# Eight orders for the up projection's matmuls and four for the down projection's, from the second tile on

## The chip, the cores and the metric

The kernel runs on one core of one Trainium2 chip. The metric is the time of one execution in microseconds of device time; lower is better. An execution consists of a linear attention (a decayed outer-product state over 768 tokens, four batches, eight heads) and, behind it, a gated feed-forward network over all 3072 tokens.

## What is computed

The reference, cut to what matters here:

```python
for t in range(S):                                   # S = 768 tokens, D = 48 channels a head
    cur = einsum('bhd,bhe->bhde', u * k[t], v[t])
    y[t] = einsum('bhd,bhde->bhe', r[t], state + cur)
    state = w * state + einsum('bhd,bhe->bhde', k[t], v[t])
x = y as (B * S, H * D)                              # 3072 x 384
gate = 1 / (1 + exp(-(x @ w_gate)))                  # 384 -> 1536
out = (gate * (x @ w_val)) @ w_out                   # 1536 -> 384
```

All of it is float32. The kernel reaches that accuracy on TensorE with a rounded type (F32R): every number is kept as a high part and a low part, and a product is three matmuls, low weights by high data, high by high, and high by low. `PASS = ((1, 0), (0, 0), (0, 1))` on line 480 lists the three as (part of the weights, part of the data).

## The kernel before

The 768 tokens are cut into 12 chunks of 64, and two chunks of the four batches make a tile of 512 columns, so there are six tiles. The attention works through 24 groups (a chunk and one half of the heads each, `GROUPS`), and each group writes its quarter of a tile's `xt`. The feed-forward network takes a tile in 12 blocks of 128 hidden units (`NF = 12`, index `f`). A block consists of

- `up(f)`, line 492: for the gate (`g = 0`) and then for the value (`g = 1`) nine matmuls (three `kt`, the thirds of the 384 inputs, by three passes) that add up in one bank of PSUM, 18 matmuls of 512 columns in all, on line 502;
- `sigmoid(f)` on ScalarE (line 511) reads the gate's bank, `product(f)` on VectorE (line 515) reads the value's bank and multiplies, `h_high(f)` on ScalarE (line 520) rounds to the high part, and `h_low(f)` on GpSimd (line 524) makes the low part;
- `down(f)`, line 532: nine matmuls (line 540) that add to three accumulators, three passes `k` by three parts of the output; in the sixth tile the third part is two pieces of 256 columns, so it has twelve.

All engines take their instructions in the order in which the program writes them. For the first tile that order stands in the string `START`. From the second tile on it is the loop at the end: for each block `i` in turn `up`, `sigmoid` and `product`; then, in the blocks that `SLOTS` names, one group of attention, `apply(n)` (line 368) and what follows it; then `h_high`, `h_low`; and then `finish(i - 1)`, the down projection of the block before. TensorE therefore sees up of block i, in 16 blocks the attention's small matmuls, down of block i - 1, up of block i + 1, and so on.

PSUM has eight banks. Two hold attention scores (`two_banks`), three the accumulators, and three are the pool `ring` (line 67), handed out in turn by `one_bank()` (line 79). `up` takes two of the ring's banks, first the gate's and then the value's, and `apply` takes two for its output:

```python
yb[n] = one_bank(), one_bank()        # line 371, in apply(n)
o = one_bank()                        # line 497, in up(f), for g = 0 and then for g = 1
```

With three banks A, B, C in turn, an up projection in A (gate) and B (value) is followed by an up projection in C and A, or, in the 16 blocks of `SLOTS`, by `apply` in C and A and then an up projection in B and C. An instruction that writes a bank waits until the last reader of the bank's former content is done. The first small matmul of `apply` writes the first of its two banks and the second one the other (`from_state`, through `into_y` on line 320). The slots are `f` = 4, 6, 8, 10 in the second tile and `f` = 1, 4, 7, 10 in the third to the fifth; the sixth has none.

Of the kernel before, what the change touches and what calls it, by code (L numbers as in the profile page):

```python
# [18 lines left out]
DM, DF = H * D, 1536  # L19
P = 128  # L20
# [3 lines left out]
NF = DF // P  # L24
# [33 lines left out]
def rwkv_then_moe(ctx: ExitStack, tc: tile.TileContext, wd, ch, tk, rt, ut, wt, rk0, vn0, wd0, out):  # L58
    nc = tc.nc
# [16 lines left out]
    def two_banks():  # L76
        return ps.tile([P, 2, 512], F32, name="sc")

    def one_bank():
        return ring.tile([P, 512], F32, name="ring")  # L80
# [12 lines left out]
    w = wu[:, 0]  # L93
# [162 lines left out]
    xt, dec, ga, yb, kv = {}, {}, {}, {}, {}  # L256
# [223 lines left out]

    PASS = ((1, 0), (0, 0), (0, 1))

    class Moe:
        def __init__(self, x, acc, cols, last=None):
            self.x, self.acc, self.cols = x, acc, cols
            c = self.cols
            self.parts = [(0, acc[0], c, c), (1, acc[1], c, c), (2, acc[2], c, c)]
            if last is not None:
                left, right = slice(0, CT), slice(CT, 2 * CT)
                self.parts[2:] = [(2, acc[2], left, left), (2, last, left, right)]  # L490
            self.pair, self.sg, self.h = {}, {}, {}

        def up(self, f):
            w = whi[f], wlo[f]
            self.pair[f] = []
            for g in range(2):
                o = one_bank()
                self.pair[f].append(o)
                k = 0
                for kt in range(3):  # L500
                    for a, b in PASS:
                        nc.tensor.matmul(  # L502
                            o[:, self.cols], w[a][:, g * DM + kt * P : g * DM + (kt + 1) * P],
                            self.x[:, kt, b, self.cols], start=(k == 0), stop=(k == 8),
                        )
                        k += 1

        def sigmoid(self, f):
            c, sg = self.cols, hp.tile([P, 512], F32, name="sg")
# [22 lines left out]
        def down(self, f):  # L532

            h, w = self.h.pop(f), (whi[f], wlo[f])
            todo = [(k, part) for k in range(3) for part in self.parts]
            if f == NF - 1:
                todo = [(k, part) for part in self.parts for k in range(3)]
            for k, (d, acc, to, cols) in todo:
                a, b = PASS[k]
                nc.tensor.matmul(  # L540
                    acc[:, to], w[a][:, 2 * DM + d * P : 2 * DM + (d + 1) * P],
                    h[:, b, cols], start=(f == 0 and k == 0 and self.cols.start == 0),
                    stop=(f == NF - 1 and k == 2),
                )

    def accumulators():
        return [pacc.tile([P, 512], F32, name=f"acc{d}") for d in range(3)]
# [35 lines left out]
    moes, accs = {}, {}  # L583

    def moe_of(it):
        ti, h, f = it
        if ti not in accs:
            accs[ti] = accumulators()
        if (ti, h) not in moes:
            cols = (slice(0, CT), slice(CT, 2 * CT), slice(0, 2 * CT))[h]  # L590
            last = two_banks()[:, 0] if ti == len(TILES) - 1 else None
            moes[ti, h] = Moe(xt[ti], accs[ti], cols, last)
        return moes[ti, h]

    def finish(i):
        ti, h, f = items[i]
        moe_of(items[i]).down(f)
        if f == NF - 1:
            if ti == len(TILES) - 1:
                store_last(moe_of(items[i]), TILES[ti][0])  # L600
            else:
                store(accs[ti], slice(TILES[ti][0], TILES[ti][-1] + 1))
# [13 lines left out]
        "o0v": lambda j: rest_of_weights(0, HALVES[j], nc.vector),  # L616
        "Rv": lambda n: queries(n, nc.vector), "Tv": lambda n: token_keys(n, nc.vector),
        "qv": lambda i: moe_of(items[i]).h_low(items[i][2], nc.vector),
        "U": lambda i: moe_of(items[i]).up(items[i][2]),
        "g": lambda i: moe_of(items[i]).sigmoid(items[i][2]),  # L620
# [4 lines left out]
    for step in START.split():  # L625
        name, _, arg = step.partition(".")
# [3 lines left out]
    last = len(GROUPS) - 1  # L630
# [18 lines left out]
    for i in range(n0, len(items)):  # L649
        ti, h, f = items[i]  # L650
# [44 lines left out]
    with tc.If(bad != 0):  # L695
        with ExitStack() as g:
# [65 lines left out]
            x = gp.tile([P, 3, 2, 512], F32R, name="xgr")  # L762
# [116 lines left out]
```

## Time and profile before

| what | value |
|---|---|
| runs of the kernel | 539.41, 539.42 and 540.52 us, median 539.42 |
| profiled execution, first to last instruction | 538.6 us |
| TensorE busy with matmuls | 519.2 us, 96% |
| TensorE loading weights (beside matmuls) | 426.9 us, 79% |
| VectorE, ScalarE, GpSimd busy | 218.3, 171.8, 175.0 us |
| matmuls of line 502 (up) | 1332, of which 1260 have 512 columns |
| matmuls of line 540 (down) | 666 |

The profiled execution's span is 0.8 us below the median of the timed runs. Busy time of TensorE is modelled: a matmul of 512 columns is shown 0.39 us long, but the next one starts 0.23 us after it. Where the text needs TensorE's pace it takes the time that 18 or 9 matmuls in a row occupy in the chain of waits, not the shown duration. `xN` behind a row is the number of instructions in it; a row of several begins with the first one's start and ends with the last one's end.

### The profile page before, as it was taken

What the parts mean: (1) busy time and instruction counts of PE and PEld (TensorE: products, weight loads), DVE (VectorE), ACT (ScalarE), POOL (GpSimd) and SP (SyncE); (2) the same over time, 40 slices, a digit from 0 to 9 for tenths busy, and PEclk for the clock granted to TensorE, in tenths of its full rate; (3) what the DMA queues carried; (4) which work ended last, traced back from release to release, by engine and by line L of the source; (5) the groups of instructions that cost most, each with busy time, mean ns of one, the idle gap of its engine ahead of it and who ended that gap; (6) DMA issues with size and microseconds to landing.
All of it is one profiled execution on the core that took longest, in us unless ns stands there. A gap on an engine that the chain in (4) does not pass through costs nothing.

```text
span 538.6 us, 12067 instructions
## 1 busy us (share of the span) xinstructions
PE 519.2 (96%) x5268; PEld 426.9 (79%) x5268; DVE 218.3 (41%) x379; ACT 171.8 (32%) x358; POOL 175.0 (32%) x156
## 2 busy tenths in 40 slices
PE   4879999999999999999999999999999999999996
PEld 3769878788788887888888888888888887888885
DVE  7798999942343342432423414313414311111111
ACT  5576654522132232231332222222322212221121
POOL 3353330002814444234145144144242311111120
PEclk9999999999999999999999999999999999999999
DMA  8886903053022213220303402203300001100001
GB/s 324 314 301 239 382 2 99 16 204 128 2 86 86 70 48 141 85 84 3 95 3 104 145 7 79 67 28 106 144 1 16 12 1 19 60 0 1 0 1 63
DMA packets 15707, 48.03 MB, mean 89 GB/s; under 512 B 2369, under 2 KB 5057, under 8 KB 14241
## 3 DMA queue, kind: packets, MB, share of 16 engines
q1 hardware_dynamic: 15360, 46.81, 25.2%
q8 instruction: 43, 0.70, 0.5%
q10 hardware_dynamic: 288, 0.39, 0.2%
q14 instruction: 16, 0.12, 0.1%
HBM read 40.12 MB, written 4.72 MB: 83 GB/s over the span
## 4 chain that ended last, share of the span: by engine, by line
PE 91%; DVE 4%; DMA 3%; ACT 1%; issue 0%; SPq 0%; DVEq 0%; ACTq 0%
PE ring L502 55%; PE acc L540 27%; PE ring L320 5%; PE sc L348 2%; DMA toks<-in_tk 1%; DMA chan<-in_ch 1%; PE sc L403 1%; DMA wr<-in_wt 1%; DVE score L362 1%; PE sc L540 1%; DVE wf L243 1%; DVE wf L244 1%; DVE wx L253 0%; ACT wf L236 0%; DVE wf L242 0%
## 5 line engine op out<-in xcount | busy, mean ns | idle before, releaser
L502 PE MATMUL ring<-xt,wx 128*128 128x512 f32 (+1 forms) x1332 | 317.1, 392 | 2.1 <-ACT wx L250 1.7
L502 PEld LDWEIGHTS ring<-xt,wx 128*128 128x128 f32 x1332 | 247.4, 191 | 57.5 <-ACT wx L250 1.9
L524 POOL TENSOR_TENSOR h<-sg,h 128x512 fp32r<-128x512 f32 (+1 forms) x68 | 91.8, 1350 | 332.4 <-ACT h L520 326.5
L540 PE MATMUL acc<-h,wx 128*128 128x512 f32 (+1 forms) x666 | 160.9, 383 | 0.0
L515 DVE TENSOR_TENSOR sg<-ring,sg 128x512 f32<-128x512 f32 (+1 forms) x74 | 50.0, 676 | 272.7 <-PE ring L502 272.7
L540 PEld LDWEIGHTS acc<-h,wx 128*128 128x128 f32 x666 | 119.6, 188 | 24.3
L511 ACT ACTIVATE sg<-ring 128x512 f32<-128x512 f32 (+1 forms) x74 | 43.4, 586 | 181.2 <-PE ring L502 181.2
L520 ACT CAST h<-sg 128x512 fp32r<-128x512 f32 (+1 forms) x74 | 45.3, 612 | 109.0 <-DVE sg L515 109.0
L422 ACT ACTIVATE state<-state,every 112x96 f32<-112x96 f32 x80 | 23.5, 363 | 26.7 <-PE ring L320 26.7
L460 DVE TENSOR_TENSOR xt<-ring,xt 112x256 fp32r<-112x256 f32 (+1 forms) x52 | 19.9, 418 | 26.9 <-ACT xt L456 26.9
L301 POOL TENSOR_TENSOR dec<-chan,every 128x512 f32<-128x512 f32 x20 | 23.8, 1190 | 13.8 <-PE ring L320 5.9
L362 DVE COPY_PREDICATED score<-masks,sc 128x512 f32<-128x512 int32 x32 | 23.8, 743 | 0.9
L456 ACT CAST xt<-ring 112x256 fp32r<-112x256 f32 (+1 forms) x52 | 17.1, 372 | 17.2 <-PE ring L320 15.6
L320 PE MATMUL ring<-score,toks 64*64 64x64 f32 (+1 forms) x768 | 18.6, 230 | 4.0 <-DVE score L362 2.0
L311 POOL TENSOR_TENSOR toks<-toks,tabn 128x384 f32<-128x384 f32 x18 | 19.7, 1093 | 0.0
L320 PEld LDWEIGHTS ring<-score,toks 64*48 64x48 f32 (+1 forms) x768 | 15.3, 133 | 5.2 <-POOL dec L301 1.9
L250 ACT CAST wx<-wf 128x1152 fp32r<-128x1152 f32 (+1 forms) x13 | 14.1, 1084 | 15.1 <-DVE wf L244 15.1
L244 DVE SCALAR_TENSOR_TENSOR wf<-wr,wf 128x1152 int32<-128x1152 int32 (+1 forms) x13 | 18.4, 1415 | 0.5
L320 PEld LDWEIGHTS ring<-dec,state 48*48 48x48 f32 (+1 forms) x704 | 12.0, 127 | 7.4 <-issue 6.7
L348 PE MATMUL sc<-dec,chan 48*64 48x64 f32 x768 | 17.6, 231 | 0.1
L289 POOL TENSOR_TENSOR dec<-dec,toks 128x384 f32<-128x384 f32 x16 | 16.3, 1016 | 1.2
L243 DVE SCALAR_TENSOR_TENSOR wf<-wr,wf 128x1152 int32<-128x1152 int32 (+1 forms) x13 | 16.5, 1266 | 0.5
(62 smaller groups left out, 253.0 us busy)
## 6 DMA issues: line engine op xcount, KB each, us to landing
wr<-in_wt SPq DMA_DIRECT2D x11, 1152.0 KB, 8.7
chan<-in_ch SPq DMA_DIRECT2D x24, 512.0 KB, 4.5
toks<-in_tk SPq DMA_DIRECT2D x24, 400.0 KB, 4.9
out_y<-wf SPq DMA_DIRECT2D x16, 256.0 KB, 2.3
dec<-in_rt SPq DMA_DIRECT2D x16, 192.0 KB, 2.6
xt<-xt SPq DMA_DIRECT2D x30, 64.0 KB, 2.3
wr<-in_wt SPq DMA_DIRECT2D x2, 576.0 KB, 5.2
xt<-xt SPq DMA_DIRECT2D x12, 32.0 KB, 4.9
```

The source lines that it names most:

```text
L244: nc.vector.scalar_tensor_tensor(g, low, 29, g, ALU.logical_shift_right, ALU.bitwise_or)
L301: eng.tensor_tensor(v4(t[:, 0]), v4(chan[n][:, 0]), bc2(table_of(n)), ALU.mult)
L320: nc.tensor.matmul(yb[n][bank][64 * half : 64 * half + m, cs], lhsT, rhs, start=first, stop=stop, skip_group_check=True,)
L348: nc.tensor.matmul(sc[64 * gm : 64 * gm + 64, be ^ gm, o : o + C], kk[row, cs : cs + C], rr[row, cs : cs + C], start=True, stop=True,)
L362: nc.vector.copy_predicated(t.rearrange("q (b m i) -> q b m i", b=2, m=4), masks[:, m].bitcast(I32).unsqueeze(1).unsqueeze(1).broadcast_to ...
L422: nc.scalar.activation(st[:, p, s], st[:, p, s], AF.Copy, scale=pw[0:112, 4 * g + 2 * p + s, 64:65],)
L502: nc.tensor.matmul(o[:, self.cols], w[a][:, g * DM + kt * P : g * DM + (kt + 1) * P], self.x[:, kt, b, self.cols], start=(k == 0), stop=(k ...
L511: nc.scalar.activation(sg[:, c], self.pair[f][0][:, c], AF.Sigmoid)
L515: nc.vector.tensor_tensor(sg[:, c], self.pair.pop(f)[1][:, c], sg[:, c], ALU.mult)
L520: nc.scalar.copy(out=h[:, 0, c], in_=sg[:, c])
L524: eng.tensor_tensor(h[:, 1, c], self.sg.pop(f)[:, c], h[:, 0, c], ALU.subtract)
L540: nc.tensor.matmul(acc[:, to], w[a][:, 2 * DM + d * P : 2 * DM + (d + 1) * P], h[:, b, cols], start=(f == 0 and k == 0 and self.cols.start ...
```

## The change

`up` and `down` no longer fix the order of their matmuls. `up_order(kind)` lists the 18 matmuls of an up projection as (g, kt, pass) in one of eight orders, `down_order(kind, parts)` the matmuls of a down projection as (pass, part) in one of four. Each matmul, its weights, its data and its bank are the same as before; the first one into a bank in the new order carries `start`, the last one `stop`. Both banks of an up projection are taken at its beginning, in the same order as before.

The first tile keeps kind 0, the old order. From the second tile on the kinds change from block to block:

| tile (ti) | up kinds, f = 0 to 11 | down kinds, f = 0 to 11 | blocks with attention |
|---|---|---|---|
| 1 | 3 4 5 6 7 0 1 2 3 4 5 6 | 2 1 2 2 3 3 0 0 1 1 2 1 | 4, 6, 8, 10 |
| 2 | 6 7 0 1 2 3 4 5 6 7 0 1 | 2 2 3 3 0 0 1 1 2 2 3 1 | 1, 4, 7, 10 |
| 3 | 1 2 3 4 5 6 7 0 1 2 3 4 | 2 3 0 0 1 1 2 2 3 3 0 1 | 1, 4, 7, 10 |
| 4 | 4 5 6 7 0 1 2 3 4 5 6 7 | 0 0 1 1 2 2 3 3 0 0 1 1 | 1, 4, 7, 10 |
| 5 | 7 0 1 2 3 4 5 6 7 0 1 2 | 2 1 2 2 3 3 0 0 1 1 2 1 | none |

Up kinds 0, 2 and 3 do the whole gate before the value. Kinds 1, 4, 5, 6 and 7 mix the two: the gate's last matmul is then the 17th of the 18 in kinds 1, 5 and 6, the 16th in kind 7 and the 15th in kind 4, where it was the ninth. Down kind 0 is pass by pass, kind 1 part by part (the last block of a tile had that before and keeps it), kinds 2 and 3 are pass by pass with the passes in the orders 1, 0, 2 and 2, 1, 0. In kind 3 the low part of `h` is read first, in kind 1 by the third matmul, in kinds 0 and 2 by the last third.

```diff
+    def up_order(kind):
+        G, K = range(2), range(3)
+        if kind == 1:
+            return [(g, kt, p) for kt in K for p in PASS for g in G]
+        if kind == 2:
+            return [(g, kt, p) for g in G for p in PASS for kt in K]
+        if kind == 3:
+            return [(g, kt, p) for g in G for kt in K for p in PASS[::-1]]
+        if kind == 4:
+            return [(g, kt, p) for kt in K for g in G for p in PASS]
+        if kind == 5:
+            one = ((0, PASS[0]), (0, PASS[1]), (1, PASS[0]), (1, PASS[1]), (0, PASS[2]), (1, PASS[2]))
+            return [(g, kt, p) for kt in K for g, p in one]
+        if kind == 6:
+            return [(g, kt, p) for ps_ in (PASS[:2], PASS[2:]) for kt in K for g in G for p in ps_]
+        if kind == 7:
+            return [(g, kt, p) for ps_ in (PASS[:1], PASS[1:]) for kt in K for g in G for p in ps_]
+        return [(g, kt, p) for g in G for kt in K for p in PASS]
+
+    def down_order(kind, parts):
+        if kind == 1:
+            return [(k, part) for part in parts for k in range(3)]
+        ks = {2: (1, 0, 2), 3: (2, 1, 0)}.get(kind, (0, 1, 2))
+        return [(k, part) for k in ks for part in parts]
+
+    UP_OF = [[0] * NF] + [[(f + 3 * ti) % 8 for f in range(NF)] for ti in range(1, 6)]
+    DOWN_OF = [[0] * NF] + [[(f // 2 + ti) % 4 for f in range(NF)] for ti in range(1, 6)]
...
         def up(self, f):
             w = whi[f], wlo[f]
-            self.pair[f] = []
-            for g in range(2):
-                o = one_bank()
-                self.pair[f].append(o)
-                k = 0
-                for kt in range(3):
-                    for a, b in PASS:
-                        nc.tensor.matmul(
-                            o[:, self.cols], w[a][:, g * DM + kt * P : g * DM + (kt + 1) * P],
-                            self.x[:, kt, b, self.cols], start=(k == 0), stop=(k == 8),
-                        )
-                        k += 1
+            self.pair[f] = [one_bank() for _ in range(2)]
+            seen_g = [0, 0]
+            for g, kt, (a, b) in up_order(UP_OF[self.ti][f]):
+                nc.tensor.matmul(
+                    self.pair[f][g][:, self.cols], w[a][:, g * DM + kt * P : g * DM + (kt + 1) * P],
+                    self.x[:, kt, b, self.cols], start=(seen_g[g] == 0), stop=(seen_g[g] == 8),
+                )
+                seen_g[g] += 1
...
         def down(self, f):
             h, w = self.h.pop(f), (whi[f], wlo[f])
-            todo = [(k, part) for k in range(3) for part in self.parts]
+            kind = DOWN_OF[self.ti][f]
             if f == NF - 1:
-                todo = [(k, part) for part in self.parts for k in range(3)]
+                kind = 1
+            elif f == 0 and kind:
+                kind = 2
+            todo = down_order(kind, self.parts)
```

## Rows read from the trace of the kernel before

**Rows 1.** The page: TensorE's busy time, granted clock by slices, and the chain's shares.
```profile
PE 519.2 (96%) x5268; PEld 426.9 (79%) x5268; DVE 218.3 (41%) x379; ACT 171.8 (32%) x358; POOL 175.0 (32%) x156
...
PEclk9999999999999999999999999999999999999999
...
PE 91%; DVE 4%; DMA 3%; ACT 1%; issue 0%; SPq 0%; DVEq 0%; ACTq 0%
```

**Rows 2.** Waits from 110 us on, longest first: who waited for whom, us, times, longest.
```profile
POOL h L524 <- ACT h L520: 300.4, 60, 38.3
DVE sg L515 <- PE ring L502: 269.4, 61, 5.6
ACT sg L511 <- PE ring L502: 172.8, 61, 3.6
...
PEld ring L320 <- issue: 6.2, 17, 0.4
```

**Rows 3.** The chain of waits from 262 to 304 us: start, duration, what.
```profile
266.51 2.05 PE acc L540 x9
268.57 4.19 PE ring L502 x18
...
274.81 4.20 PE ring L502 x18
279.01 0.61 PE ring L320 x28
...
293.71 2.05 PE acc L540 x9
```

**Rows 4.** The timeline of a block with attention, 253.5 to 263 us.
```profile
253.70 4.36 PE L502 MATMUL ring<-xt,wx 128*128 128x512 f32 x18
256.05 0.60 ACT L511 ACTIVATE sg<-ring 128x512 f32<-128x512 f32 x1 [2.79 <-PE ring L502]
257.99 0.54 PEld L320 LDWEIGHTS ring<-dec,state 48*64 48x64 f32 x32 [0.37 <-issue]
257.99 0.68 PE L320 MATMUL ring<-dec,state 48*64 48x64 f32 x32
258.17 0.69 DVE L515 TENSOR_TENSOR sg<-ring,sg 128x512 f32<-128x512 f32 x1 [5.56 <-PE ring L502]
...
260.55 0.76 DVE L460 TENSOR_TENSOR xt<-ring,xt 112x256 fp32r<-112x256 f32 x2 [1.57 <-ACT xt L456]
...
261.39 1.30 POOL L524 TENSOR_TENSOR h<-sg,h 128x512 fp32r<-128x512 f32 x1 [6.76 <-ACT h L520]
...
262.16 1.09 PE L502 MATMUL ring<-xt,wx 128*128 128x512 f32 x4
```

**Rows 5.** The timeline of the next block, without attention, 263 to 276.9 us.
```profile
266.35 2.22 PE L540 MATMUL acc<-h,wx 128*128 128x512 f32 x9
266.62 0.69 DVE L515 TENSOR_TENSOR sg<-ring,sg 128x512 f32<-128x512 f32 x1 [2.54 <-PE ring L502]
...
268.04 1.30 POOL L524 TENSOR_TENSOR h<-sg,h 128x512 fp32r<-128x512 f32 x1 [5.35 <-ACT h L520]
...
268.40 4.36 PE L502 MATMUL ring<-xt,wx 128*128 128x512 f32 x18
...
272.60 2.22 PE L540 MATMUL acc<-h,wx 128*128 128x512 f32 x9
```

**Rows 6.** The timeline around 39 us: TensorE waits there for ScalarE.
```profile
37.83 1.15 ACT L250 CAST wx<-wf 128x1152 fp32r<-128x1152 f32 x1 [0.68 <-DVE wf L244]
...
38.99 0.30 PEld L502 LDWEIGHTS ring<-xt,wx 128*128 128x128 f32 x2 [1.85 <-ACT wx L250]
39.02 0.47 PE L502 MATMUL ring<-xt,wx 128*128 128x256 f32 x2 [1.68 <-ACT wx L250]
```

**Rows 7.** Three up matmuls in a row, from the timeline at 514 us.
```profile
513.72 0.87 PE L502 MATMUL ring<-xt,wx 128*128 128x512 f32 x3
```

**Rows 8.** Busy time by stretches: us, PE busy (instructions), granted clock, DMA share, GB/s.
```profile
36.00:39.20 3.20, 1.52 (x15) 1.00 0.46 107
39.40:42.70 3.30, 3.30 (x16) 0.50 0.94 360
```

**Rows 9.** The timeline of the end, from 528 us on.
```profile
530.95 0.69 DVE L524 TENSOR_TENSOR h<-sg,h 128x512 fp32r<-128x512 f32 x1 [0.69 <-ACT h L520]
...
531.40 1.90 PE L540 MATMUL acc<-h,wx 128*128 128x512 f32 x9
```

More of the change, by code (lines that the diff above doesn't have):

```diff
@@ L481, in rwkv_then_moe, with __init__ @@
     PASS = ((1, 0), (0, 0), (0, 1))
+    def up_order(kind):
[23 more added lines that the diff above has]
+    DOWN_OF = [[0] * NF] + [[(f // 2 + ti) % 4 for f in range(NF)] for ti in range(1, 6)]
     class Moe:
-        def __init__(self, x, acc, cols, last=None):
-            self.x, self.acc, self.cols = x, acc, cols
+        def __init__(self, x, acc, cols, last=None, ti=0):
+            self.x, self.acc, self.cols, self.ti = x, acc, cols, ti
             c = self.cols
@@ L534, in down @@
             h, w = self.h.pop(f), (whi[f], wlo[f])
-            todo = [(k, part) for k in range(3) for part in self.parts]
+            kind = DOWN_OF[self.ti][f]
             if f == NF - 1:
-                todo = [(k, part) for part in self.parts for k in range(3)]
-            for k, (d, acc, to, cols) in todo:
+                kind = 1
+            elif f == 0 and kind:
+                kind = 2
+            todo = down_order(kind, self.parts)
+            begin = [i for i, t in enumerate(todo) if id(t[1]) not in [id(u[1]) for u in todo[:i]]]
+            end = [i for i, t in enumerate(todo) if id(t[1]) not in [id(u[1]) for u in todo[i + 1 :]]]
+            for i, (k, (d, acc, to, cols)) in enumerate(todo):
                 a, b = PASS[k]
@@ L541, in down @@
                     acc[:, to], w[a][:, 2 * DM + d * P : 2 * DM + (d + 1) * P],
-                    h[:, b, cols], start=(f == 0 and k == 0 and self.cols.start == 0),
-                    stop=(f == NF - 1 and k == 2),
+                    h[:, b, cols], start=(f == 0 and i in begin and self.cols.start == 0),
+                    stop=(f == NF - 1 and i in end),
                 )
@@ L591, in moe_of @@
             last = two_banks()[:, 0] if ti == len(TILES) - 1 else None
-            moes[ti, h] = Moe(xt[ti], accs[ti], cols, last)
+            moes[ti, h] = Moe(xt[ti], accs[ti], cols, last, ti)
         return moes[ti, h]
```

## The prediction, made before the changed kernel ran

> **What bounds the kernel now.** I read the page first. TensorE is busy 96% of the span, the chain that ended last is 91% TensorE, and the granted clock is full in every slice [rows 1]. Then the waits: from 110 us on, where the changed blocks lie, the long ones are other engines waiting for TensorE; of TensorE only its weight loader appears, 6.2 us over 17 times with the releaser "issue", that is, waiting for nothing that the trace shows [rows 2]. Then the chain in a stretch of steady work: an up projection of 18 matmuls takes 4.19 us, a down projection 2.05 us, the attention's matmuls stand between some of them, and one piece begins where the last ends [rows 3]. So the time is the sum of TensorE's instructions, nothing else is on the path, and an order of matmuls can matter in two ways only: it changes the pace, or it makes TensorE wait for somebody.
>
> **The pace.** The change issues the same matmuls with the same weight loads, so only the spacing could move. The trace holds two orders of the down projection. The nine matmuls at 266.51 us go pass by pass, each into another bank than the one before; those at 293.71 us belong to a tile's last block and go part by part, three in a row into one bank with the passes in turn, as an up projection of kind 0 does for each `kt`. Both take 2.05 us, 0.228 a matmul [rows 3]. Alternating banks or staying in one, keeping the data or changing it made no difference there. The up projection takes 4.19 / 18 = 0.233 us a matmul [rows 3] under the same sequence of passes, so I lay its 0.005 us to what it reads and writes, not to the order. I take 0 for the new orders. Bounds: 53 up projections have a kind other than 0 (60 less 7). If all went at the down projection's pace, each would take 2 x 2.05 = 4.10 us, 0.09 less, 4.8 us in all. The other way, three up matmuls at 514 us stand (0.87 - 0.39) / 2 = 0.24 us apart [rows 7]; at that spacing throughout, 0.007 x 18 x 53 = 6.7 us more. The 33 full-width down projections whose order changes would, at the up projection's pace, cost 9 x 0.233 - 2.05 = 0.05 us each, 1.6 us more.
>
> **The gate that ends late, and the bank that attention takes.** In kinds 0, 2 and 3 the gate is complete after nine matmuls, and sigmoid runs while the value's nine are on TensorE. Take the attention block of [rows 4]: the up projection begins at 253.70 us, sigmoid runs from 256.05 to 256.65, the last value matmul starts at 253.70 + 4.36 - 0.39 = 257.67, and the first small matmul of `apply` starts at 257.99. `apply` needs two of the ring's three banks. The first was last read by the product of the block before. The second is the bank of this block's gate, so the second small matmul must wait for this block's sigmoid; before the change that had been over for 1.3 us.
>
> In the mixed kinds it is not over. How long sigmoid starts after the gate's last matmul starts: the ninth starts at 253.70 + 8 x 0.233 = 255.56, sigmoid at 256.05, so 0.49 us; its duration is 0.60 [rows 4]. From ScalarE's end to TensorE's weight load: the cast at 37.83 ends at 38.98 and the load starts at 38.99, its matmul at 39.02 [rows 6]; I take 0.03 us. In kinds 1, 5 and 6 the gate's last matmul is the 17th of 18 and starts at 257.67 - 0.23 = 257.44. Sigmoid ends at 257.44 + 0.49 + 0.60 = 258.53, and the second small matmul goes at 258.56 instead of 257.99: 0.57 us, of which the other bank's first matmul hides nothing. In kind 7 the gate's last is the 16th, 0.23 us earlier: 0.34 us. Kind 4 would pay 0.11, but no attention block has it.
>
> Counting by the table of kinds, the attention blocks with a mixed kind are: second tile f = 4 (kind 7), 6 (1), 10 (5); third tile f = 1 (7), 7 (5); fourth tile f = 4 (5); fifth tile f = 1 (5), 10 (6). That is six at 0.57 and two at 0.34: 3.4 + 0.7 = 4.1 us. Queued behind the waiting matmul is all of TensorE: the rest of `apply`, the down projection, the next up projection. TensorE is the path, so nothing gives this back. Bounds for one wait: not below 0, and not above 0.80, which it would be if sigmoid started only after the last of the 18 matmuls.
>
> **The mixed blocks without attention.** There are 39 mixed blocks in all, so 31 of these. There the next up projection takes the gate's bank, and with a mixed order of its own needs it at its second matmul rather than its tenth. But a down projection lies between. In [rows 5] the down projection starts at 266.35 and the next up projection at 268.40; a gate that ended one matmul before 266.35 - 0.23 = 266.12 gives sigmoid until 265.89 + 0.49 + 0.60 = 266.98, so 1.4 us are left. I cost it at 0; without that cover each would cost what an attention block does.
>
> The Trainium skill ("Perfetto Trace Analysis", Optimizing Tensor Performance, Matmuls) asks that independent matmul groups rotate through PSUM banks so that reading one out overlaps the next group's matmuls. A mixed order ends both groups together, so by that rule as it stands all 39 mixed blocks would lose the overlap; the trace agrees only where no other matmuls fill the gap.
>
> **After an attention block** the next up projection's second group goes into the first bank of `apply`, which `x_low` reads last. Its two instructions end at 261.31 and the up projection starts at 262.16 [rows 4], so 0.85 us are left even for an order that touches that bank at once. A delayed `apply` moves both alike. Cost 0.
>
> **The hidden values.** The product now waits for sigmoid: it starts at about 0.89 us after the last matmul instead of 258.17 - 257.67 = 0.50 [rows 4], and h's low part comes up to 0.4 us later. It ends at 262.69 for a down projection that starts at 266.35 [rows 4, 5], and in the block after at 269.34 for one at 272.60 [rows 5]. With 3.2 us to spare, a down order that reads the low part first (kind 3) or third (kind 1) costs 0 too; the spare is what would be lost first.
>
> **The end.** The last block's up kind is 2, gate first, and its down order is the one it had. Its low part is done at 531.64, and the third matmul of the last down projection, the first to read it, starts at 531.40 + 2 x 0.233 = 531.87 [rows 9]. Nothing of it moves. Tile starts: the first block of a tile still begins with `kt` = 0, whose data comes first. Cost 0.
>
> **The sum.** Profiled execution 538.6 + 4.1 - 0.1 for the rounding of the steps (the waits are more likely a little under than over, since the first small matmul may start on its own) = 542.6 us of span; the timed runs lie 0.8 us above the span, so 543.4 us against a median of 539.42.
>
> **The rivals.**
>
> 1. *The up projections speed up.* If what holds them at 0.233 us is a property of the old order after all, the 53 changed ones gain up to 0.09 each: 543.4 - 4.8 = 538.6, not slower. It decides from 4.0 / 53 = 0.075 us per projection. For it: the two kinds of projection do differ in pace. Against: the two down orders do not [rows 3].
> 2. *No wait.* If the ring gave `apply` another bank than the gate's, or sigmoid were taken up earlier, the time stays 539.4. Against: three banks in turn leave no other.
> 3. *Everybody pays.* If the reading of the gate's bank held TensorE up in every mixed block, as the page's rule has it, 39 blocks at about 0.5 us are 20 us: 559. Against: the 1.4 us of cover [rows 5].
> 4. *The pace falls.* Changed down projections at the up projection's pace give 543.4 + 1.6 = 545.0; up projections at 0.24 us a matmul give 550. Against: as under 1.
> 5. *The clock falls.* After a pause of some 1.6 us in 36 to 39.2 the granted clock is 0.50, the lower level of 1.2 GHz, from 39.4 to 42.7 [rows 6, 8]. If a wait of 0.57 us did the same, a stretch of 3.3 us at half pace would cost 1.6 us, and eight of them 13 us: 556. Against: the new waits are a third as long, and the matmuls on either side are dense.
>
> **How the numbers follow.** The forecast has 0.70, with a range of its own from 542.2 to 544.6 (eight waits of 0.35 to 0.65). Rival 1 has 0.10, rival 2 0.07, rival 3 0.03, rival 4 0.08 (most of it near 545), rival 5 0.02. The range from 541.0 to 545.8 holds the forecast, the milder half of rival 4 and some partial gain of pace, and leaves about 0.2 out. A change of less than 0.2% (538.3 to 540.5) can't be told from none here. Slower by more: 0.70 + 0.03 + 0.08 + 0.02, less a little for waits that come out small, 0.79. Within: rival 2 and half of rival 1, 0.12. Faster: the rest of rival 1 and what I overlook, 0.09.
>
> **What would show it.** Right: in the waits of the changed kernel's attention matmuls (line 320) on sigmoid (line 511) stand about eight times, 0.3 to 0.6 us, 4 us in all, in just the eight blocks named, and an up projection still takes 4.19 us and a down projection 2.05. Wrong: an up projection of a changed kind at another length; waits of up or down matmuls (lines of the new `up` and `down`) on ScalarE, VectorE or GpSimd; a granted clock below 1.00 after 110 us; or no waits on sigmoid at all.

## The result, and the profile after

| kernel | timed runs, us | median | ratio to before, 95% interval |
|---|---|---|---|
| before | 539.41 to 540.52 (4) | 539.83 | |
| with the change | 545.18 to 546.83 (4) | 545.72 | 1.0095 [1.0068, 1.0122] |

The change makes the kernel slower, by 3.7 to 6.6 us; forecast were 4.0 (543.4 us in a range of 541.0 to 545.8). The profiled execution's span went from 538.6 to 543.3 us.

The page after the change, the lines that answer to [rows 1]: busy time by engine, and the chain's shares by engine and by line.

```profile
PE 520.9 (96%) x5268; PEld 427.2 (79%) x5268; DVE 218.7 (40%) x379; ACT 171.6 (32%) x358; POOL 174.6 (32%) x156
...
PE 90%; DVE 4%; issue 2%; DMA 2%; ACT 1%; SPq 1%; POOL 0%; ACTq 0%; POOLq 0%; DVEq 0%
PE ring L526 55%; PE acc L569 27%; PE ring L320 5%; PE sc L348 2%; DMA chan<-in_ch 2%; PE sc L403 1%; DVE xt L460 1%; PE sc L569 1%; ACT sg L535 1%; DVE wf L243 1%; DVE wx L253 0%; DVE sg L539 0%; DVE score L362 0%; SPq L105 0%; DVE wf L242 0%
```

TensorE has the same 5268 matmuls. What is new is sigmoid (now line 535) with 1% of the chain. The waits from 110 us on, the lines with TensorE or its weight loader in front (as [rows 2]: total, times, longest):

```profile
PEld ring L320 <- issue: 6.2, 17, 0.4
...
PEld ring L320 <- ACT sg L535: 2.7, 8, 0.4
...
PE ring L320 <- ACT sg L535: 1.5, 6, 0.3
...
PEld sc L348 <- POOL dec L301: 0.4, 1, 0.4
...
PEld ring L213 <- DVE good L211: 0.4, 1, 0.4
```

The last two stand in the view of before too (0.4 us each). The eight waits of the weight loader for sigmoid are the eight forecast. The view counts only the time in which the engine shows nothing at all; what a wait costs is read from the timeline. Here is the block whose rows before were [rows 4] (third tile, f = 7, kind 5):

```profile
256.00 4.36 PE L526 MATMUL ring<-xt,wx 128*128 128x512 f32 x18
...
260.22 0.60 ACT L535 ACTIVATE sg<-ring 128x512 f32<-128x512 f32 x1 [4.66 <-PE ring L526]
260.29 0.19 PEld L320 LDWEIGHTS ring<-dec,state 48*64 48x64 f32 x2 [0.37 <-issue]
260.29 0.32 PE L320 MATMUL ring<-dec,state 48*64 48x64 f32 x2
260.85 0.69 DVE L539 TENSOR_TENSOR sg<-ring,sg 128x512 f32<-128x512 f32 x1 [5.94 <-ACT sg L535]
260.87 0.48 PEld L320 LDWEIGHTS ring<-dec,state 48*64 48x64 f32 x27 [0.39 <-ACT sg L535]
260.87 0.62 PE L320 MATMUL ring<-dec,state 48*64 48x64 f32 x27 [0.26 <-ACT sg L535]
```

Sigmoid starts as the up projection's 18 matmuls end and no longer in their middle. Two instructions go at 260.29, 4.29 us after the up projection began, as before (257.99 - 253.70); each small matmul of `from_state` is two instructions in the trace (16 in the program, 32 in [rows 4]), so this is the first one. The rest, which in [rows 4] followed in the same row, waits and stands in a row of its own from 260.87 on, 0.58 us later. In the chain the two projections keep their lengths (the answer to [rows 3]; at 265.21 stands an up projection of kind 6, at 271.46 one of kind 7, at 269.40 a down projection of kind 1):

```profile
260.22 0.61 ACT sg L535
...
262.94 2.27 PE acc L569 x9
265.21 4.19 PE ring L526 x18
269.40 2.05 PE acc L569 x9
271.46 4.19 PE ring L526 x18
```

Worked out from the starts of all matmuls after 112 us in the two traces: the 16 stretches of attention grew by 4.12 us together (0.57 six times, 0.34 twice, the other eight by less than 0.005), the 60 up projections by 0.00 us and the 60 down projections by 0.07 us together. That is 4.2 of the 4.7 us by which the spans differ. The other 0.5 lies before 112 us, where nothing was changed; there the traces of e1 to e6, e8, e9 and e11 below lie between 1.2 us less and 0.8 us more than the one of before.

### The profile page after: what moved, and what is told of

It is laid out like the page before. It is cut to its first block, busy times and chain, and to the rows that moved or that the text cites. A ratio compares the mean times of both kernels' runs of the same rounds, so it can differ in the third digit from the quotient of the medians.

```text
span 543.3 us, 12067 instructions
## 1 busy us (share of the span) xinstructions
PE 520.9 (96%) x5268; PEld 427.2 (79%) x5268; DVE 218.7 (40%) x379; ACT 171.6 (32%) x358; POOL 174.6 (32%) x156
## 4 chain that ended last, share of the span: by engine, by line
PE 90%; DVE 4%; issue 2%; DMA 2%; ACT 1%; SPq 1%; POOL 0%; ACTq 0%; POOLq 0%; DVEq 0%
PE ring L526 55%; PE acc L569 27%; PE ring L320 5%; PE sc L348 2%; DMA chan<-in_ch 2%; PE sc L403 1%; DVE xt L460 1%; PE sc L569 1%; ACT sg L535 1%; DVE wf L243 1%; DVE wx L253 0%; DVE sg L539 0%; DVE score L362 0%; SPq L105 0%; DVE wf L242 0%
## 5 line engine op out<-in xcount | busy, mean ns | idle before, releaser
L548 POOL TENSOR_TENSOR h<-sg,h 128x512 fp32r<-128x512 f32 (+1 forms) x68 | 90.3, 1328 | 335.8 <-ACT h L544 335.8
L456 ACT CAST xt<-ring 112x256 fp32r<-112x256 f32 (+1 forms) x52 | 17.1, 372 | 15.4 <-PE ring L320 13.8
L320 PEld LDWEIGHTS ring<-dec,state 48*48 48x48 f32 (+1 forms) x704 | 13.4, 127 | 10.2 <-issue 6.5
L320 PEld LDWEIGHTS ring<-score,toks 64*64 64x64 f32 (+1 forms) x768 | 15.5, 133 | 4.7 <-POOL dec L301 1.9
L320 PE MATMUL ring<-dec,state 48*48 48x64 f32 (+1 forms) x704 | 17.5, 223 | 1.6 <-ACT sg L535 1.5
L244 DVE SCALAR_TENSOR_TENSOR wf<-wr,wf 128x1152 int32<-128x1152 int32 (+1 forms) x13 | 18.4, 1416 | 0.5
L348 PEld LDWEIGHTS sc<-dec,chan 48*64 48x64 f32 x768 | 15.9, 145 | 2.3 <-issue 1.1
```

Of the source, the lines that this page charges most:

```text
L320: nc.tensor.matmul(yb[n][bank][64 * half : 64 * half + m, cs], lhsT, rhs, start=first, stop=stop, skip_group_check=True,)
L348: nc.tensor.matmul(sc[64 * gm : 64 * gm + 64, be ^ gm, o : o + C], kk[row, cs : cs + C], rr[row, cs : cs + C], start=True, stop=True,)
L548: eng.tensor_tensor(h[:, 1, c], self.sg.pop(f)[:, c], h[:, 0, c], ALU.subtract)
```

## The experiments

The theory: the whole loss is the attention's second bank, which waits for sigmoid. All ratios are to the kernel before, run on the same chip (medians 540.55, 540.72 and 540.83 us in the three groups); the difference in microseconds is the ratio's.

| run | ratio, 95% interval | us | forecast |
|---|---|---|---|
| e1_attention_blocks_old_order | 1.0000 [0.9981, 1.0019] | 0.0 | 0 to 0.5 |
| e2_only_the_eight | 1.0062 [1.0039, 1.0085] | +3.4 | +4.1 |
| e3_all_sixteen_kind_1 | 1.0165 [1.0141, 1.0188] | +8.9 | +9.2 |
| e4_all_others_kind_1 | 1.0006 [0.9987, 1.0026] | +0.3 | 0 |
| e5_scores_before_state | 1.0165 [1.0141, 1.0189] | +8.9 | +0.6 |
| e6_gate_in_second_bank | 0.9997 [0.9981, 1.0014] | -0.2 | +14 |
| e7_data_moved_128_bytes | 0.9858 [0.9833, 0.9883] | -7.7 | -6 or 0 |
| e8_all_sixteen_kind_4 | 1.0029 [1.0012, 1.0045] | +1.6 | +1.8 |
| e9_down_before_attention | 1.0006 [0.9985, 1.0027] | +0.3 | 0 to 0.5 |
| e10_change_and_data_moved | 0.9943 [0.9923, 0.9964] | -3.1 | -3.5 |
| e11_turn_kept_gate_second | 1.0285 [1.0256, 1.0313] | +15.4 | +14 |
| e12_data_moved_64_bytes | 1.0017 [0.9998, 1.0035] | +0.9 | -7 or less gain |

**Which blocks cost.** Five runs take the change apart by blocks.

```diff
 # e1, behind UP_OF
+    for ti, fs in SLOTS.items():
+        for f in fs:
+            UP_OF[ti][f] = 0
 # e2 (mixed kinds only in SLOTS; DOWN_OF all 0)
+    UP_OF = [[(f + 3 * ti) % 8 if f in SLOTS.get(ti, ()) and (f + 3 * ti) % 8 not in (2, 3) else 0 ...
 # e3 (DOWN_OF all 0); e8 has 4 * (f in SLOTS.get(ti, ()))
+    UP_OF = [[int(f in SLOTS.get(ti, ())) for f in range(NF)] for ti in range(6)]
 # e4 (DOWN_OF all 0)
+    UP_OF = [[int(ti > 0 and f not in SLOTS.get(ti, ())) for f in range(NF)] for ti in range(6)]
```

> The change with the 16 attention blocks' up projections put back to kind 0; all other up and all down projections keep their new orders. Theory (the loss is the eight waits of the attention for sigmoid): none of them is left, the time is that of before, 0 to +0.5 us. Rival 3 (every mixed block pays): 31 mixed blocks are left at about 0.1 us or more each, +3 us or more. Rival 4 (the pace of the new orders): 37 changed up projections and 42 changed down projections are left, so most of the loss, +3 us.

> Only the eight up projections that are mixed and stand before attention take their new order; every other up projection and all down projections keep the old one. Theory: the whole loss, +4.1 us (six waits of 0.57 and two of 0.34). Rivals 3 and 4: only the eight blocks' part of it, under +1 us.

> All 16 up projections before attention take kind 1, everything else the old order. Theory: 16 waits of 0.57 us, +9.2 us, each in apply's second matmul. If what the change lost is not proportional to the number of such blocks (a clock that falls, a delay that is partly given back later), it differs from this by more than 1 us.

> All 44 up projections with no attention behind them take kind 1, the 16 before attention and all down projections the old order. Theory: the down projection between covers sigmoid with 1.4 us to spare, so 0 +- 0.4 us. Rival 3 (every mixed block pays): 44 blocks at 0.5 us, +22 us. Rival 4 (pace): at 0.24 us a matmul +5 us, at the down projection's pace -4 us.

> All 16 up projections before attention take kind 4, in which the gate's last matmul is the 15th of 18; everything else the old order. Theory: sigmoid ends two matmuls (0.47 us) earlier than in kind 1, so each wait is 0.57 - 0.47 = 0.11 us, +1.8 us in all. If a mixed order has a price of its own beside the end of the gate, it is more, near +9 us at the worst.

With the attention blocks back in the old order nothing of the loss is left, though 40 up (37 was a miscount) and 42 down projections keep new orders (e1). The eight blocks alone bring it (e2; its interval of 2.1 to 4.6 us holds 4.1, and its trace has the same 4.12 us in the same eight stretches). Sixteen bring 16 times 0.57 (e3: every stretch of attention but two longer by 0.573 to 0.575 us, the last two by 0.54 and 0.57). Kind 4 brings what the end of its gate says, 0.11 a block (e8). Of the 44 mixed blocks without attention 42 cost nothing in the trace of e4, which takes rival 3 away, and with it the Trainium skill's rule (Perfetto Trace Analysis, Optimizing Tensor Performance, Matmuls) in the sense that a lost overlap always costs. The other two show where the cover does end. One is the second block of the second tile (`f` = 1). GpSimd makes its low part and then, in order, the queries (line 301) that the first group's scores need. The rows of before, and those of e4 behind them:

```profile
136.02 1.19 POOL L301 TENSOR_TENSOR dec<-chan,every 128x512 f32<-128x512 f32 x1
...
137.35 0.56 PEld L348 LDWEIGHTS sc<-dec,chan 48*64 48x64 f32 x32 [0.37 <-POOL dec L301]
```

```profile
135.84 1.19 POOL L301 TENSOR_TENSOR dec<-chan,every 128x512 f32<-128x512 f32 x1
...
137.08 0.56 PEld L348 LDWEIGHTS sc<-dec,chan 48*64 48x64 f32 x32 [0.68 <-POOL dec L301]
```

Before, the queries were ready 0.14 us ahead (136.02 + 1.19 against 137.35); in e4 the scores wait for them, 0.31 us by the starts of the matmuls. In the change this block has kind 4 and the scores come no later than before. The other is the last block, of kind 1 in e4: at the end of the kernel the low part is late. The matmul that reads it waits:

```profile
531.04 0.69 DVE L548 TENSOR_TENSOR h<-sg,h 128x512 fp32r<-128x512 f32 x1 [0.69 <-ACT h L544]
...
531.79 1.36 PEld L569 LDWEIGHTS acc<-h,wx 128*128 128x128 f32 x7 [0.43 <-DVE h L548]
```

Worked out from the matmuls' starts that end is 0.35 us longer. In the change the last block has kind 2, and its end is as long as before.

**Is it the bank?** Three runs leave the orders and change what lies between, or which bank it is.

```diff
 # e9 (e3 and this)
         if attend:
+            finish(i - 1)
             more = GROUPS[n][0] < NC - 1
...
-        finish(i - 1)
+        if not attend:
+            finish(i - 1)
 # e6 (UP_OF and DOWN_OF all 0); e11 has this and the next, and bufs=1 for the pool
             self.pair[f] = [one_bank() for _ in range(2)]
+            if self.ti:
+                self.pair[f].reverse()
 # e11
+    banks = []
...
-        return ring.tile([P, 512], F32, name="ring")
+        banks.append(len(banks) % 3)
+        return ring.tile([P, 512], F32, name="ring", tag=f"ring{banks[-1]}")
```

> As the run with kind 1 in all 16 attention blocks (+9 us), but in these blocks the down projection of the block before goes to TensorE ahead of apply and not behind it. The work is the same; the down projection's 2.06 us now lie between the gate's end and apply's second bank. Theory: sigmoid is over 1.5 us before it is asked for, all 16 waits go, 0 to +0.5 us against before. The next up projection's second bank is then short of the 2 us of cover that it had behind apply, but as it is of kind 0 it asks for that bank 2.1 us after it begins. Rival (a mixed order before attention costs time in itself): +9 us stay.

> All orders as before the change; only from the second tile on the value takes the first of an up projection's two banks and the gate the second, so that apply's second bank is the value's. Theory (the bank is what is waited for): apply's second matmul now waits for the product, which ends 0.50 + 0.69 us after the last value matmul starts, 0.89 us after apply could go; 16 times 0.89 is +14 us. Rival (the wait belongs to the mixed order, not to the bank): 0 us, since no order is changed.

> The run with the gate in the second bank again, now with the ring's three banks handed out strictly in turn (three tags of one bank each). In the earlier run the pool had given apply whichever bank was released first, which is the gate's wherever it lies, so the edit did not do what it was meant to. Now apply's second bank is the value's, last read by the product. All orders are the old ones. Theory: each of the 16 attention blocks waits for the product, which ends 0.50 + 0.69 us after the last value matmul starts; 1.22 less the 0.33 after which apply could go is 0.89, 16 times is +14 us. Rival (only mixed orders wait): 0 us.

With the down projection in between, the same 16 mixed blocks cost nothing that the runs can tell (e9; in its trace the attention has its old length again). e6 missed. The reason, as I read it from the program's allocation, which no view of the profile shows: the pool does not hand its banks out in turn, as I had written, but gives the one that was released first. The gate's bank is released before the value's, so `apply` got the gate's bank in all 16 blocks of e6 too; in the kernel before and in the change the two rules come to the same. The runs bear this out: e6 and e11 differ only in how the banks are handed out. With the turn enforced by tags (e11) `apply` gets the value's bank, and without any change of order TensorE waits for the product (here line 544):

```profile
263.04 0.33 PE L323 MATMUL ring<-dec,state 48*64 48x64 f32 x2
...
263.22 0.69 DVE L544 TENSOR_TENSOR sg<-ring,sg 128x512 f32<-128x512 f32 x1 [5.56 <-PE ring L531]
...
263.96 0.48 PEld L323 LDWEIGHTS ring<-dec,state 48*64 48x64 f32 x27 [0.74 <-DVE sg L544]
263.96 0.62 PE L323 MATMUL ring<-dec,state 48*64 48x64 f32 x27 [0.60 <-DVE sg L544]
```

What followed at once in [rows 4] goes at 263.96 in place of 263.04, 0.92 us later, where 0.89 were forecast. So the wait belongs to the bank and its last reader; a mixed order is neither needed for it nor enough.

**A cover that was somebody else's.**

```diff
 # e5, in apply (the change and this)
+            early = n >= FIRST and n + 1 < len(GROUPS)
+            if early:
+                scores(n + 1)
+                if GROUPS[n][0] < NC - 1:
+                    outer(n, ga[n + 1][:, :, 256:512])
             from_state(n)
-            if n < FIRST or n + 1 == len(GROUPS):
+            if not early:
                 nc.tensor.drain()
             else:
-                scores(n + 1)
-                if GROUPS[n][0] < NC - 1:
-                    outer(n, ga[n + 1][:, :, 256:512])
```

> The whole change, and in apply the next group's scores and outer products, which need no bank of the ring, go to TensorE ahead of the matmuls that write the ring's banks (15 of the 16 attention blocks; the last group has none). In the trace of before these are 0.87 us of work. Theory: the work covers the wait of 0.57 us, so seven of the eight waits go and one (fifth tile, f = 10, 0.57 us) stays: +0.6 us against before. If TensorE waits for sigmoid for another reason than the ring's bank, the waits move to the first score matmuls and the +4 us stay.

e5 missed. The waits from 110 us on:

```profile
PEld ring L320 <- DVE seen L383: 6.5, 15, 0.4
...
PEld sc L348 <- issue: 4.5, 12, 0.4
...
PE ring L320 <- DVE seen L383: 4.4, 15, 0.3
...
PEld ring L320 <- ACT sg L537: 0.4, 1, 0.4
```

The waits for sigmoid went as expected, all but the last group's one. But in the old order the scores and outer products lie between `from_state` and the last matmuls of `apply`, which wait until VectorE has copied a column of both banks (`seen`, line 381 of the kernel before). Moved ahead, they no longer cover that. Now all 15 moved groups wait, 14 of them 0.58 us and one 0.44, where the change had seven waits there.

**The pace.** The prediction laid the difference of 0.233 and 0.228 us a matmul to what is read. By the sizes of the tiles all weights and hidden values begin at the same address of a partition modulo 512 bytes, and `xt` 384 bytes beside it (of what lies between, only the three `toks` tiles, 9600 bytes together, are no multiple of 512).

```diff
 # e7, e10 (the change and this)
-    table = const.tile([P, 1], F32, name="table")
+    table = gains[1][:, 0:1]
-        total = const.tile([1, 1], F32, name="total")
+        total = good[0:1, 0:1]
+    shift = main.enter_context(tc.tile_pool(name="shift", bufs=1))
+    shift.tile([P, 32], F32, name="pad")        # e12: [P, 16]
     xp = main.enter_context(tc.tile_pool(name="xp", bufs=2))
```

> The kernel before with the tiles of x moved in SBUF by 128 bytes against the weights, so that x, the weights and the hidden values begin at the same address modulo 512 (as only the weights and the hidden values did); two small scratch tiles share another's place. No order is changed. The question is what sets the up projection's 0.233 us a matmul against the down projection's 0.228, which the prediction laid to what is read. If it is the relative address, an up projection takes 18 x 0.227 = 4.09 us in place of 4.19 and the time falls by 0.1 x 60 = 6 us; if not, 0 us.

> The moved kernel with x moved by 64 bytes and not by 128: x then begins at 448 modulo 512 relative to the weights, before at 384, in the faster kernel at 0. If any distance other than 384 is good, or any move, 4.08 us an up projection and -7 us; if x has to lie at the same address modulo 512 (or 128) as the weights, the up projection stays above 4.08 us and the gain is smaller or none.

> The whole change together with x moved by 128 bytes. If the pace depends on where x lies and not on the order of the matmuls, all eight up orders now take 4.08 us a projection, as the moved kernel's one order did, and the two effects add: -7.6 + 4.1 = -3.5 us against before. The waits grow a little, since sigmoid's end is fixed and the matmuls behind the gate's last are 0.006 us shorter each. If some orders have another pace, up projections of different kinds differ in length.

The chain of e7 at 285 us, and that of e12 and of e10 behind it (an up projection each, and a down projection):

```profile
285.19 4.08 PE ring L504 x18
289.27 2.04 PE acc L542 x9
```

```profile
285.18 4.20 PE ring L504 x18
289.38 2.06 PE acc L542 x9
```

```profile
281.37 4.08 PE ring L528 x18
285.45 2.04 PE acc L571 x9
287.49 4.08 PE ring L528 x18
```

At distance 0 an up projection falls to 4.08 us, exactly two down projections; at 384 it is 4.19 and at 448 4.20. Worked out from the starts, 6.4 us of e7's gain lie in the 60 up projections and 0.6 in the down projections. e12 shares the same small tiles as e7 and gains nothing, so the gain is the address and not the sharing. Weights and hidden values keep their distance in all these runs and only x moves against them; whether its distance to the weights counts or its own address is not shown. With the change on top (e10) the two up projections shown are of kind 1; in every other kind the matmuls are 0.227 us apart too, and the eight waits are back. e7 beats both kernels: 531.76 to 534.28 us.

## Why the prediction was right

- **The pace, taken as unchanged: right.** No kind of either projection differs by more than 0.01 us in the mean. Its reason was tested too: e7 moves the pace without touching an order, and e10 has one pace under all orders. Rivals 1 and 4 fall with that.
- **The wait of the attention's second bank, six times 0.57 and two times 0.34: right** in place, number and size (0.57 and 0.34 in the trace). e1 to e3 and e8 show the dose, e11 the bank. The step's reason had a fault: the banks don't go in turn but by release. It changed nothing here and cost e6.
- **Mixed blocks without attention at 0: right** (e1, e4); the cover named, the down projection, is what counts (e9).
- **The second bank after attention, the hidden values, the end, the tile starts at 0: right;** no wait of an up or down matmul stands in the trace after 110 us. For the hidden values it was luck in part: the step asked only whether the low part comes in time for the down projection (3.2 us to spare) and not what GpSimd does behind it. Before the first group's scores 0.14 us were to spare, and e4 lost 0.31 there; the change loses nothing because its table has kind 4 in that block.
- **The clock (rival 5): it did not fall.** The granted clock is 1.00 (the level of 2.4 GHz) in the stretches after the change, waits of 0.57 us included:

```profile
200.00:300.00 100.00, 99.72 (x904) 1.00 0.24 73
300.00:400.00 100.00, 99.49 (x1021) 1.00 0.24 77
```

- **The sum** came out 4.1 against 4.2 in the trace after 112 us; the timed runs say 3.7 to 6.6. The 0.8 us that I added from the span to the timed runs is no property of the kernel: it sets the span of one execution against the median of others. In every run whose span is on record the time lies 1.7 to 2.0 us above the span of the same execution (here 545.18 and 543.3), so the profiled execution of before was one of its slower ones, at some 540.5 us by that, and the forecast comes to the median of before plus 4.0. The measured median, 545.72, lies above the prediction's narrower range (542.2 to 544.6) and 0.1 us inside the wide one; that it is still inside is luck. Whether the waits have a part in what exceeds 4.2 us the timed runs don't show. The trace has no more of them, e2 with the same eight waits measured +3.4, and the stretch before 112 us, which the change does not touch, differs between the traces by up to 2 us.

## What to carry to other kernels

Ask of a reordering first who reads each bank last and who writes it next: an order that ends two accumulations together costs only where the next writer of a bank follows at once, and then by the reader's end, which two timeline rows give. Ask the same of the engines that stand behind the late reader in order: in e4 the loss came through GpSimd. Before work is moved to cover a wait, look what it covers where it stands (e5). And compare the pace of matmuls of the same shape: where two lines differ by a few per cent in every block, the addresses of their operands are worth one run.

## What the runs showed of the hardware that was not expected

In these runs the spacing of matmuls of 512 columns depends on where the streamed data lie in a partition. With data and weights at the same address modulo 512 it is 0.227 us without any pattern; with x 384 bytes off, 0.233, alternating between 0.238 and 0.229; 448 bytes off, 0.233 to 0.234. These are worked out from the starts of the matmuls in the traces of e7, before and e12. In the order of matmuls, banks, passes and reuse of the data nothing of it could be found, in eight and four orders. Whether the period is 512 or 256 was not tried; 128 is ruled out, since 384 is a multiple of it. Nor was it tried whether the distance to the weights counts or the data's own address, since the weights were never moved against the hidden values.

The Trainium skill (TensorE: Matmul & The Clock Gate, Back-to-back issue gap) gives 512 / 2.4 + 2.5, 216 ns, for an isolated matmul, which no run here has; the best stream here, with a weight load for every matmul, has 227 ns.
